# The last output tile of a spectral-mixing and MLP-mixer kernel: its products, sums, transposes and stores in another order and on three DMA queues

## The chip, the cores and the metric

The kernel runs on one core of a Trainium2 chip. The metric is device time in microseconds (us) for one execution; the number given for a kernel is the median of several unprofiled executions. A separate execution was profiled; its span runs from its first instruction to its last, and times inside it are counted from the span's start. Engines are named as the profile names them: PE is TensorE's matrix multiply and PEld its weight load, DVE is VectorE, ACT is ScalarE, POOL is GpSimd, SP is SyncE. A "q" after the name stands for the engine's sequencer: what it issues itself, such as DMAs and semaphore waits.

## The reference

```python
X = np.fft.rfft(x, axis=1)                      # x: 8 x 3008 x 256, fp32
y = np.fft.irfft(X * (filt_r + 1j * filt_i)[None], n=3008, axis=1)
h = np.maximum(y.transpose(0, 2, 1) @ w_tok1, 0.0) @ w_tok2     # token mixing
u = y + h.transpose(0, 2, 1)
out = u + np.maximum(u @ w_ch1, 0.0) @ w_ch2    # channel mixing, 256 -> 1536 -> 256
```

A filter in the frequency domain along the sequence is followed by an MLP over the 3008 tokens and an MLP over the 256 channels, each with a residual. All of it is fp32.

## The kernel before, in words

The Fourier transforms are products with small tables, done for groups of one or two batches (`GROUPS`). Their steps are a generator, `dft`, which the main loop advances at fixed places beside the mixer of an earlier batch, so that TensorE always has products to do. In the last batch there is no such work left.

The mixer (`mix`) goes over 8 batches, 6 tiles of tokens each (`MT`; the last tile of a batch has 448 tokens, the others 512) and 6 pairs of hidden channel blocks each (`JP`). One of these is an item `(b, m, jp)`. Products of 2 x 2 blocks are done with seven products in place of eight, so half-widths (256 or 224) and sums before and after appear everywhere. The loop is a software pipeline of depth two: in step `i` the first half of the channel MLP of item `i` (`up_first`, `up_middle`, `up_last`, the ReLU on ScalarE) stands between parts of the second half of item `i - 1` (`h_sums`, `down`). The instructions of each engine run in the order in which they are written, and waits on semaphores between engines come from the buffers that the instructions share.

`down` (L967 to L979) makes the seven products of an item in three parts, each of the form `po[i][:, j] += chan * mov`. Four PSUM banks `po[0]` to `po[3]`, each with two halves `j`, collect them over the six items of a tile. In the last item of a tile the order is (0,0), (0,1), (2,0), then (1,1), (3,0), then (2,1), (1,0). The operands are the ReLU's output `hh` and three kinds of sums of it, `t`, which VectorE makes in three operations (`h_sums`, through `v` at L922).

When a tile's last item is done, `finish` (L981 to L1029) adds the banks to the residual `u` (the tile `ut`, 2 x 448 or 2 x 512 per partition). It copies one half bank with ScalarE (L990) and makes eight additions on VectorE (`a`, `b_`, `c`, `d`). Two `transpose` instructions (L1010), one for each half of the channels (`dh`), turn 32 x 32 blocks into the tile `r`. The function `store` (L1012) then writes `r` with 16 DMAs (L1025): for `h` in 0, 1 (which of two token ranges), `e` in 0, 1 and `g` in 0 to 3 (blocks of 32 partitions). In every tile but the last of the last batch these are issued by GpSimd. In the last one SyncE and ScalarE issue eight each:

```python
last = b == B - 1 and m == MT - 1
q = (nc.sync, nc.scalar)[g % 2] if last else nc.gpsimd
```

For the very last tile there is no next item, so `down`, `finish` and `store` of it run with nothing beside them. After the program's last instruction come its end steps, which the profile puts at L1286, the line of the launch: SyncE waits for all DMAs and engines, each engine drains, GpSimd gathers the others in a barrier, semaphores are cleared, and a second barrier follows.

Of the kernel before, what the change touches and what calls it, by code (L numbers as in the profile page):

```python
# [10 lines left out]
FP32 = mybir.dt.float32  # L11
# [6 lines left out]
B = 8  # L18
N = 3008
N1 = 47  # L20
N2 = 64
NF = N // 2 + 1
D = 256
P = 128
K2 = 32
A = 24
KR = 4 * A
KH = KR // 2
HALF = 64
# [14 lines left out]
DH = D // P  # L44
CW = 32
CB = P // CW
MT = 6
# [80 lines left out]
def kernel(  # L128
# [11 lines left out]
    nc = tc.nc  # L140
# [19 lines left out]
    def pool(name, bufs, **kw):  # L160
        return ctx.enter_context(tc.tile_pool(name=name, bufs=bufs, **kw))
# [13 lines left out]
    tp = pool("tp", 2)  # L175
    vp = pool("vp", 2)
    sp = pool("sp", 1)
    rp = pool("rp", 1)
# [35 lines left out]
    chan = []  # L214
# [621 lines left out]
    def width(m):  # L836
        return 512 if m < MT - 1 else 448
# [83 lines left out]
    def v(out, in0, in1, op=ALU.add):  # L921
        nc.vector.tensor_tensor(out=out, in0=in0, in1=in1, op=op)  # L922

    def sums(t, b12_22, b11_12, b11, b21):

        return (lambda: v(t[:, 0:2], b12_22, b11_12, ALU.subtract),
                lambda: v(t[:, 2], t[:, 1], b11),
                lambda: v(t[:, 3], t[:, 2], b21, ALU.subtract))
# [6 lines left out]
    def h_sums(hh, t, w):  # L935

        h = hh[:, :, 0:w // 2]
        return sums(t[:, :, 0:w // 2], h[:, 1:3], h[:, 0:2], h[:, 0], h[:, 3])
# [28 lines left out]
    def down(m, jp, part, hh, t, po):  # L967
# [9 lines left out]
        for i, j, first, last, n, mov in todo[part]:  # L977
            nc.tensor.matmul(po[i][:, j, 0:hw], chan[1][:, jp, n, :], mov, start=(jp == 0 and first == 1),  # L978
                             stop=(jp == JP - 1 and last == 1))  # L979

    def finish(b, m, ut, po):  # L981

        w = width(m)
        hw = w // 2
        us = ut[:, :, 0:w].rearrange("p d (s n) -> p d s n", s=2)
        p23, p45, p16, p7 = (v_[:, :, 0:hw] for v_ in po)
        r = rp.tile([P, 512 // CW, DH, CW], FP32, tag="r", name="r")
        flat = r.rearrange("p k d i -> p (k d i)")
        p1, u2, u3 = (flat[:, ds(256 * i, hw)] for i in range(3))
        nc.scalar.copy(out=p1, in_=p16[:, 0])  # L990

        def a():
            v(us[:, 0], p23, us[:, 0])
            v(u2, p16[:, 1], p1)

        def b_():
            v(us[:, 1], p45, us[:, 1])
            v(us[:, 0, 1], p45[:, 1], us[:, 0, 1])
            v(u3, p7[:, 0], u2)

        def c():
            v(us[:, 0, 0], us[:, 0, 0], p1)
            v(us[:, 0, 1], us[:, 0, 1], u2)

        def d():
            v(us[:, 1], us[:, 1], u3.unsqueeze(1).to_broadcast([P, 2, hw]))

        def turn(dh):

            nc.vector.transpose(r[:, 0:w // CW, dh, :], ut[:, dh, 0:w].rearrange("p (k i) -> p k i", i=CW))  # L1010

        def store():  # L1012
            turn(1)
            ob = out[b]
            cw = DH * CW
            blocks = r.rearrange("p (q h e) d i -> p h e q (d i)", h=2, e=2)
            for h in range(2):
                n = min(4, (w - h * HALF + HALF) // P)
                for e in range(2):
                    for g in range(CB):  # L1020

                        last = b == B - 1 and m == MT - 1
                        q = (nc.sync, nc.scalar)[g % 2] if last else nc.gpsimd
                        row = e * 32 * N1 + (A + 4 * m if h else A - 1 - 4 * m)
                        q.dma_start(bass.AP(tensor=ob.tensor, offset=ob.offset + row * D + g * cw,  # L1025
                                            ap=[[N1 * D, 32], [D if h else -D, n], [1, cw]]),
                                    blocks[ts(g, CW), h, e, 0:n])

        return [a, b_, c, d, lambda: turn(0), store]  # L1029

    h1s, uts, vts = {}, {}, {}
# [22 lines left out]
    def mix(next_ready):  # L1054

        wait = []
        pos, hhs, tts = {}, {}, {}

        def loads(b):
            if b + 1 < B and next_ready(b):  # L1060
                for c in wait:
                    t4_load(b + 1, c)
                wait.clear()


        own = ({(4, 2): (0, 1)}, {(2, 2): (0,), (3, 0): (1,), (3, 2): (2, 3)})
        new = {(JP - 2, 0): (0, 1), (JP - 1, 0): (2, 3)}

        def u_parts(b, m, jp, place):
            parts = own[b > 0] if m + 1 < MT else new if b + 1 < B else {}  # L1070
            now = parts.get((jp, place), ())
            b, m = (b, m + 1) if m + 1 < MT else (b + 1, 0)
            for part in now:
                u_part(b, m, part)
            if now and now[-1] == max(p for ps in parts.values() for p in ps):
                if m:
                    wait.append(m)
                todo_v.extend(v_steps(b, m))
                if b and (b, m) < (B - 1, MT - 2):
                    w2m_load((m + 2) % MT)  # L1080

        to_dram = [f for m in range(MT) for f in w2_sums(m)]
        w1_todo, w1_out = w1_sums()
        items = [(b, m, jp) for b in range(B) for m in range(MT) for jp in range(JP)]
        n = MT * JP
        for i in range(len(items) + 1):
            now, old = i < len(items), i >= 1
            if JP - 2 <= i < JP + 2:
                for _ in range(6 if i > JP - 2 else 1):
                    if w1_todo:  # L1090
                        w1_todo.pop(0)()
            elif i >= 2 * JP and i % 2 and w1_out:
                w1_out.pop(0)()
            if i and ended[0] < len(tiles):
                convert_middle()
                convert_end(False)
                convert_middle()
            if now:
                b, m, jp = items[i]
                if i % n == 0:  # L1100
                    wait.append(0)
                w = width(m)
                hhs[i] = hp.tile([P, 4, 256], FP32, tag="hh", name="hh")
                g = [bank("pg").rearrange("p (s n) -> p s n", s=2) for _ in range(2)]
                s = up_first(jp, uts[b, m], vts[b, m], w, g)
                up_middle(hhs[i], w, g, s)
            while todo_h1:
                todo_h1.pop()()
            if i < n:
                one_step()  # L1110
            if old:
                bo, mo, jo = items[i - 1]
                tts[i - 1] = tp.tile([P, 4, 256], FP32, tag="t", name="t")
                for f in h_sums(hhs[i - 1], tts[i - 1], width(mo)):
                    f()
                down(mo, jo, 0, hhs[i - 1], tts[i - 1], pos.setdefault((bo, mo), []))
            if now:
                u_parts(b, m, jp, 0)
            copies()
            yield b, i % n, 0  # L1120
            if ended[0] < len(tiles):
                if i == 0:
                    convert_middle()
                convert_end(False)
            if now:
                up_last(jp, uts[b, m], vts[b, m], w, g, s, hhs[i])
                if b + 1 < B and i % n == n - 4:
                    t4_sums(b + 1, 0)
            one_step()
            if i >= n or i % n == n - 1:  # L1130
                one_step()
            if now and b + 1 < B:
                if n - 4 - W1S <= i % n < n - 4:
                    w1_load(i % n - (n - 4 - W1S))
                if i % n == n - 4:
                    t4_sums(b + 1, 1)
            copies()
            loads(b)
            yield b, i % n, 1
            if old:  # L1140
                down(mo, jo, 1, hhs[i - 1], tts[i - 1], pos[bo, mo])
            yield b, i % n, 1.5
            if old:
                down(mo, jo, 2, hhs.pop(i - 1), tts.pop(i - 1), pos[bo, mo])
                if jo == JP - 1:
                    todo_v.extend(finish(bo, mo, uts[bo, mo], pos[bo, mo]))
                    one_step()
                    one_step()
            if now:
                if b + 1 < B and i % n == n - 4:  # L1150
                    h1s[b + 1] = token_product(b + 1)
                u_parts(b, m, jp, 2)
                if jp == JP - 1:
                    while todo_v and m + 1 == MT:
                        one_step()
                if i >= 8 and to_dram:
                    to_dram.pop(0)()
                if i in (28, 29):
                    w2m_load(i - 28)
            loads(b)  # L1160
            yield b, i % n, 2
        while todo_v:
            one_step()

    with tc.manual_schedule():
# [69 lines left out]
        n = MT * JP  # L1235
        for b, i, place in mix(next_ready):
# [9 lines left out]
            jp = i % JP  # L1246
# [44 lines left out]
```

## Time and profile before

| what | value |
|---|---|
| median of 3 unprofiled executions | 2424.17 us (2424.15 to 2425.02) |
| the profiled execution's own time | 2425.85 us |
| its span, first to last instruction | 2424.1 us |
| mean granted TensorE clock | 0.995 |
| VectorE operations of 448 elements per partition (t, u, hh) | 0.61 to 0.63 us |
| VectorE operations of 224 elements per partition | 0.38 to 0.40 us |
| ScalarE copy of 224 elements (L990) | 0.35 us |
| DMAs of the last tile | 16, 32 KB or 24 KB each |

A row of the chain of work reads: start in us, duration in us, engine, tile and line, and how many instructions were merged. In the timeline a row is: start, duration, engine, line, operation, output and input tiles, count, and in brackets the idle time before it with what ended it. In a row of stretches the numbers after the length are, for each engine, the busy time and the count, then the granted clock, the mean busy share of the 16 DMA engines and the GB/s that they moved. In a row for one line and engine the durations are least, median and most in ns, followed by the first and last start in us.

### The profile page before, as it was taken

How to read it: one execution, taken by the hardware profiler on the slowest of the kernel's cores; microseconds unless marked ns; L12 is line 12 of the kernel's file. 1: busy time of each engine (PE TensorE's matmuls, PEld its weight loads, DVE VectorE, ACT ScalarE, POOL GpSimd, SP SyncE). 2: the span in 40 equal slices, each digit the busy share in tenths (PEclk: the TensorE clock that was granted, in tenths of full speed). 3: DMA queues.
4: the chain of work that ended last, by engine and by line, in shares of the span. 5: the costliest groups of instructions: out<-in, count | busy, mean ns of one | idle time of the engine just before them, and what ended most of it. 6: DMA issues, size and time to landing. Idle time of an engine off the chain costs nothing.

```text
span 2424.1 us, 35550 instructions
## 1 busy us (share of the span) xinstructions
PE 2382.0 (98%) x12340; PEld 1985.9 (82%) x12340; DVE 1942.6 (80%) x3684; ACT 686.5 (28%) x1355; POOL 619.6 (26%) x1115
## 2 busy tenths in 40 slices
PE   7999999999999999999999999999999999999998
PEld 4666676978888888987888888897889888898887
DVE  7798778787887888777888888877787788777776
ACT  5733322232222222123222222213221222222222
POOL 7476332113111211211121112112112112112121
PEclk8999999999999999999999999999999999999999
DMA  9975545544343322444344222434324221411100
GB/s 217 248 231 166 155 144 177 161 155 138 108 133 98 86 79 78 160 134 146 103 132 125 76 81 82 145 101 133 90 75 151 63 60 46 152 63 31 39 15 20
DMA packets 187420, 278.66 MB, mean 115 GB/s; under 512 B 35485, under 2 KB 125291, under 8 KB 187240
## 3 DMA queue, kind: packets, MB, share of 16 engines
q1 hardware_dynamic: 140952, 212.56, 29.1%
q0 software_dynamic: 34688, 53.83, 8.2%
q10 hardware_dynamic: 11600, 10.00, 1.3%
q8 instruction: 98, 1.61, 0.3%
q14 instruction: 82, 0.67, 0.1%
HBM read 193.52 MB, written 82.72 MB: 114 GB/s over the span
## 4 chain that ended last, share of the span: by engine, by line
PE 90%; DVE 4%; DMA 2%; ACT 1%; issue 1%; POOL 1%; SPq 0%; ACTq 0%; DVEq 0%; POOLq 0%
PE ps_po L978 33%; PE ps_pg L944 18%; PE ps_pg L960 14%; PE ps_b L523 4%; PE ps_b L810 3%; PE ps_acc L865 3%; PE ps_acc L810 2%; PE ps_b L865 2%; PE ps_b L843 2%; PE ps_acc L843 2%; PE ps_pg L523 1%; PE ps_b L759 1%; DVE t L922 1%; DVE hh L922 1%; DMA filt<-in_x_dram 1%
## 5 line engine op out<-in xcount | busy, mean ns | idle before, releaser
L1025 POOL DMA_DIRECT2D out_dram<-r x752 | 407.9, 550 | 1542.3 <-issue 1082.2
L922 DVE TENSOR_TENSOR hh<-ps_pg,s 128x512 f32<-128x512 f32 (+3 forms) x864 | 482.0, 585 | 184.3 <-ACT s L947 181.4
L965 ACT ACTIVATE hh<-hh 128x512 f32<-128x512 f32 (+1 forms) x576 | 347.7, 621 | 993.4 <-DVE hh L922 989.5
L978 PE MATMUL ps_po<-t,wc 128*128 128x256 f32 (+1 forms) x2304 | 553.5, 379 | 1.8 <-DVE t L922 1.8
L978 PEld LDWEIGHTS ps_po<-t,wc 128*128 128x128 f32 x2304 | 427.8, 190 | 122.6 <-issue 40.8
L978 PE MATMUL ps_po<-hh,wc 128*128 128x256 f32 (+1 forms) x1728 | 413.2, 375 | 1.0 <-POOL wc L382 0.8
L944 PE MATMUL ps_pg<-v,wc 128*128 128x256 f32 (+1 forms) x1728 | 413.3, 375 | 0.7 <-POOL wc L381 0.7
L944 PEld LDWEIGHTS ps_pg<-v,wc 128*128 128x128 f32 x1728 | 327.3, 190 | 41.3 <-DVE v L922 3.1
L978 PEld LDWEIGHTS ps_po<-hh,wc 128*128 128x128 f32 x1728 | 327.7, 190 | 39.6 <-POOL wc L382 2.0
L960 PE MATMUL ps_pg<-u,wc 128*128 128x256 f32 (+1 forms) x1152 | 292.9, 377 | 1.2 <-DVE hh L922 1.2
L922 DVE TENSOR_TENSOR t<-t,hh 128x256 f32<-128x256 f32 (+1 forms) x576 | 245.0, 425 | 19.8
L960 PEld LDWEIGHTS ps_pg<-u,wc 128*128 128x128 f32 x1152 | 216.7, 190 | 44.2 <-DVE hh L922 13.9
L922 DVE TENSOR_TENSOR s<-ps_pg,hh 128x512 f32<-128x512 f32 (+1 forms) x288 | 196.1, 681 | 30.0
L947 ACT COPY s<-ps_pg 128x256 f32<-128x256 f32 (+1 forms) x288 | 105.9, 368 | 362.7 <-PE ps_pg L944 360.5
L922 DVE TENSOR_TENSOR t<-hh 128x512 f32<-128x512 f32 (+1 forms) x288 | 195.0, 677 | 0.6 <-ACT hh L965 0.6
L944 PE MATMUL ps_pg<-u,wc 128*128 128x256 f32 (+1 forms) x576 | 169.3, 375 | 2.9 <-DVE hh L922 2.8
L960 PE MATMUL ps_pg<-v,wc 128*128 128x256 f32 (+1 forms) x576 | 168.8, 375 | 0.0
L944 PEld LDWEIGHTS ps_pg<-u,wc 128*128 128x128 f32 x576 | 108.1, 190 | 19.3 <-DVE hh L922 6.2
L922 DVE TENSOR_TENSOR u<-ps_acc,u 128x256 f32<-128x256 f32 (+1 forms) x84 | 46.2, 550 | 97.0 <-PE ps_acc L865 66.1
L960 PEld LDWEIGHTS ps_pg<-v,wc 128*128 128x128 f32 x576 | 109.1, 190 | 12.7
L922 DVE TENSOR_TENSOR u<-ps_b,u 128x512 f32<-128x512 f32 (+2 forms) x126 | 74.4, 591 | 28.9 <-PE ps_b L865 26.7
L865 PE MATMUL ps_acc<-w 128*128 128x256 f32 (+1 forms) x336 | 85.5, 377 | 1.0 <-ACT t L539 1.0
(152 smaller groups left out, 2661.9 us busy)
## 6 DMA issues: line engine op xcount, KB each, us to landing
w<-w_tmp SPq DMA_DIRECT2D x84, 448.0 KB
w<-w_tmp SPq DMA_DIRECT2D x35, 896.0 KB
out_dram<-r POOLq DMA_DIRECT2D x696, 32.0 KB, 2.5
t<-g_tmp SPq DMA_DIRECT2D x42, 512.0 KB
g_tmp<-t SPq DMA_DIRECT2D x96, 192.0 KB
t<-z_tmp SPq DMA_DIRECT2D x180, 96.0 KB
z_tmp<-t SPq DMA_DIRECT2D x60, 256.0 KB
filt<-in_x_dram SPq DMA_DIRECT2D x90, 128.0 KB
```

What stands on the lines that cost most here:

```text
L523: nc.tensor.matmul(outs(i, j), stat(i, j), mov(i, j), start=True, stop=True)
L759: nc.tensor.matmul(acc[:, t, :], w1[:, a, ts(t, P)], t4[b, a // TC4][:, a % TC4, :], start=(a == 0 and t == 0), stop=(a == A - 1 and t == ...
L810: nc.tensor.matmul(ps[:, at], w[:, n], mov, start=(j == 0 and i in (0, 2)), stop=(j == AP - 1 and i >= 5))
L843: nc.tensor.matmul(ps[:, ds(q * P, n)], t4[b, c][:, r, ts(dh, P)], wai[:, 0:n], start=(first and q == 0), stop=(not first and q == 3))
L865: nc.tensor.matmul(ps[:, ds(j * hw, hw)], h1[:, n, :], w2m[m % 2][:, at, 0:hw], start=(i < 2 and j == 0), stop=(j == len(todo) - 1))
L922: nc.vector.tensor_tensor(out=out, in0=in0, in1=in1, op=op)
L944: nc.tensor.matmul(ps[:, 0:hw], chan[0][:, jp, n, :], mov, start=True, stop=True)
L947: nc.scalar.copy(out=s[:, 0], in_=g[0][:, 0, 0:hw])
L960: nc.tensor.matmul(ps[:, 0:hw], chan[0][:, jp, n, :], mov, start=True, stop=True)
L965: nc.scalar.activation(out=hs, in_=hs, func=AF.Relu)
L978: nc.tensor.matmul(po[i][:, j, 0:hw], chan[1][:, jp, n, :], mov, start=(jp == 0 and first == 1), stop=(jp == JP - 1 and last == 1))
L1025: q.dma_start(bass.AP(tensor=ob.tensor, offset=ob.offset + row * D + g * cw, ap=[[N1 * D, 32], [D if h else -D, n], [1, cw]]), blocks[ts(g ...
```

## The change

In the step after the last item, the loop calls a new function, `last_item`, and ends. The items before it, and `finish` for the other 47 tiles, are as they were; `store` only moves its DMAs into a helper, `store_piece`, with GpSimd as the queue for all of them.

`last_item` does for the very last item what `h_sums`, `down` and `finish` did, in this order. The seven products are (0,0), (0,1), (2,0), (1,1), (2,1), (3,0), (1,0). The partial sums lie in a tile `s` of the pool `sp` in place of the space of `r`. The sums on VectorE are seven operations, the first as before. The transposes are cut into eight: for each `h` and `e`, one for each `dh`, of 128 elements for `h` = 0 and 96 for `h` = 1. The four stores of a group `(h, e)` follow its two transposes. Of these, two go to one hardware queue, one to the other and one to GpSimd; in sum ScalarE and SyncE issue six each and GpSimd four.

```diff
+    def store_piece(b, m, blocks, h, e, n, queues):
+        ob = out[b]
+        cw = DH * CW
+        row = e * 32 * N1 + (A + 4 * m if h else A - 1 - 4 * m)
+        for g, q in enumerate(queues):
+            q.dma_start(bass.AP(tensor=ob.tensor, offset=ob.offset + row * D + g * cw,
+                                ap=[[N1 * D, 32], [D if h else -D, n], [1, cw]]),
+                        blocks[ts(g, CW), h, e, 0:n])
+
+    def last_item(b, m, jp, hh, t, ut, po):
+        w = width(m)
+        hw = w // 2
+        b11, b21, b22 = (hh[:, i, 0:hw] for i in (0, 3, 2))
+        t1, t3, t2, t4_ = (t[:, i, 0:hw] for i in range(4))
+
+        def times(i, j, last, n, mov):
+            nc.tensor.matmul(po[i][:, j, 0:hw], chan[1][:, jp, n, :], mov, start=False, stop=last)
+
+        for f in h_sums(hh, t, w):
+            f()
+        times(0, 0, False, 1, b21)
+        times(0, 1, True, 2, b22)
+        times(2, 0, False, 0, b11)
+        times(1, 1, False, 6, t1)
+        times(2, 1, True, 5, t2)
+        times(3, 0, True, 4, t3)
+        times(1, 0, True, 3, t4_)
+        us = ut[:, :, 0:w].rearrange("p d (s n) -> p d s n", s=2)
+        p23, p45, p16, p7 = (v_[:, :, 0:hw] for v_ in po)
+        u = sp.tile([P, 3, 256], FP32, tag="s", name="s")[:, :, 0:hw]
+        nc.scalar.copy(out=u[:, 0], in_=p16[:, 0])
+        v(us[:, 0], p23, us[:, 0])
+        v(u[:, 1], p16[:, 1], u[:, 0])
+        v(us[:, 0], us[:, 0], u[:, 0:2])
+        v(u[:, 2], p7[:, 0], u[:, 1])
+        v(us[:, 1], us[:, 1], u[:, 2].unsqueeze(1).to_broadcast([P, 2, hw]))
+        v(us[:, :, 1], us[:, :, 1], p45[:, 1].unsqueeze(1).to_broadcast([P, 2, hw]))
+        v(us[:, 1, 0], us[:, 1, 0], p45[:, 0])
+        r = rp.tile([P, 512 // CW, DH, CW], FP32, tag="r", name="r")
+        blocks = r.rearrange("p (q h e) d i -> p h e q (d i)", h=2, e=2)
+        for h in range(2):
+            n = min(4, (w - h * HALF + HALF) // P)
+            for e in range(2):
+                for dh in range(DH):
+                    rows = ut[:, dh].rearrange("p (q h e i) -> p h e q i", h=2, e=2, i=CW)
+                    nc.vector.transpose(blocks[:, h, e, 0:n, ts(dh, CW)], rows[:, h, e, 0:n])
+                hw_queues = (nc.sync, nc.scalar) if e else (nc.scalar, nc.sync)
+                store_piece(b, m, blocks, h, e, n, [hw_queues[0], hw_queues[1], nc.gpsimd, hw_queues[0]])
...
                 for e in range(2):
-                    for g in range(CB):
-
-                        last = b == B - 1 and m == MT - 1
-                        q = (nc.sync, nc.scalar)[g % 2] if last else nc.gpsimd
-                        row = e * 32 * N1 + (A + 4 * m if h else A - 1 - 4 * m)
-                        q.dma_start(bass.AP(tensor=ob.tensor, offset=ob.offset + row * D + g * cw,
-                                            ap=[[N1 * D, 32], [D if h else -D, n], [1, cw]]),
-                                    blocks[ts(g, CW), h, e, 0:n])
+                    store_piece(b, m, blocks, h, e, n, [nc.gpsimd] * CB)
...
             now, old = i < len(items), i >= 1
+            if not now:
+                bo, mo, jo = items[i - 1]
+                t = tp.tile([P, 4, 256], FP32, tag="t", name="t")
+                last_item(bo, mo, jo, hhs.pop(i - 1), t, uts[bo, mo], pos[bo, mo])
+                break
```

More of the change, by code (lines that the diff above doesn't have):

```diff
@@ L1013, in store @@
             turn(1)
-            ob = out[b]
-            cw = DH * CW
             blocks = r.rearrange("p (q h e) d i -> p h e q (d i)", h=2, e=2)
```

## The prediction

> **What bounds the kernel now.** First the page's busy times. TensorE is busy 98% of the span, so over the whole run nothing but its work counts; the change leaves all but the last seven products alone.
>
> ```profile
> PE 2382.0 (98%) x12340; PEld 1985.9 (82%) x12340; DVE 1942.6 (80%) x3684; ACT 686.5 (28%) x1355; POOL 619.6 (26%) x1115
> ```
>
> Second, the chain of work that ended last, cut to the end of the span (start us, us, what). After the last products nothing is left for TensorE, and every step is in the open.
>
> ```profile
> 2410.84 2.55 PE ps_po L978 x12
> 2413.39 0.02 issue
> 2413.41 0.35 ACT r L990
> 2413.77 0.02 issue
> 2413.79 0.39 DVE r L922
> 2414.18 0.83 DVE u L922 x2
> 2415.01 0.30 DVE r L922
> 2415.30 1.15 DVE u L922 x3
> 2416.45 0.02 issue
> 2416.47 0.65 DVE r L1010
> 2417.12 0.53 DVEq L1286
> ```
>
> Each product is two instructions here, 0.19 us apart. ScalarE's copy at 2413.41 reads only what the third product wrote, yet it waits for twelve instructions, six products: the sixth is the last into the same bank (po2), so the wait goes by bank. Then VectorE works alone until 2417.65 (2.68 us of sums, 1.17 of two transposes).
>
> Third, the timeline after that, and the busy times by stretches (the last three numbers: TensorE clock, DMA share, GB/s).
>
> ```profile
> 2417.72 3.81 ACTq L1025 DMA_DIRECT2D out_dram<-r  x8
> 2417.74 3.69 SPq L1025 DMA_DIRECT2D out_dram<-r  x8
> ```
> ```profile
> 2418.50:2420.50 2.00, 0.00 (x0) 0.00 (x0) 0.00 (x0) 0.00 (x0) 0.00 (x0) 0.56 0.63 131
> 2420.50:2422.40 1.90, 0.00 (x0) 0.00 (x0) 0.00 (x0) 0.00 (x0) 0.00 (x0) 0.50 0.51 104
> 2422.40:2424.10 1.70, 0.00 (x0) 0.00 (x0) 0.00 (x0) 0.00 (x0) 0.00 (x0) 0.50 0.00 0
> ```
>
> The stores are bound by their issue: 0.48 us each on ScalarE's queue, 0.46 on SyncE's, while the DMA engines are 63% and then 51% busy. The last issue starts at 2421.1; SyncE, done issuing at 2421.4, then waits 1.2 for a transfer, so the last lands near 2422.7, 1.65 after its issue began. 1.4 us of end-of-program steps follow (L1286, the launch line) to 2424.1.
>
> Fourth, GpSimd, which ends its own part early now. Its timeline, its end-of-program drain (ns, start us) and, for comparison, VectorE's:
>
> ```profile
> 2396.06 8.66 POOL L1025 DMA_DIRECT2D out_dram<-r  x16 [30.42 <-ACT s L947]
> ```
> ```profile
> L1286 POOLq DRAIN  x1: 9032/9032/9032, 2402.9 to 2402.9; - x1
> ```
> ```profile
> L1286 DVEq DRAIN  x1: 1207/1207/1207, 2416.5 to 2416.5; - x1
> ```
>
> The sixteen stores of the tile before are all issued by 2396.06 + 8.66 = 2404.72, the last landing 2.6 after its start at 2404.16, at 2406.7. But the drain that follows in GpSimd's order ends only at 2402.95 + 9.03 = 2411.98: 7.27 us after the last issue, 5.3 after the last landing. VectorE's drain ends 0.05 after its last transpose. Today this costs nothing, because 2411.98 lies 11 us ahead of the final barrier, in which GpSimd gathers the others (its first semaphore there: 2423.3, then 0.77 to the end).
>
> [...]
>
> **The change, part by part.** All times are in the profiled run, span 2424.1 inside 2425.85 us; the unprofiled median is 2424.17. I work with differences and add them to the median.
>
> *Order of products.* (2,1), the last into po2, moves from sixth to fifth. Its operand t2 is ready at 2411.88 (the t rows: 2411.48 and 2 x 0.41), ahead of its slot at 2410.84 + 8 x 0.19 = 2412.4, so no stall. Copy at 2413.41 - 0.38 = 2413.03, done 2413.38: **-0.38**. The bounds are 0 and -0.38.
>
> *Sums.* From the rows, an operation starts 0.53 (448 elements) or 0.30 (224) after an independent one, but 0.65 or 0.42 after one it depends on. Before, after the first sum: seven operations, 2413.79 to 2416.47, 2.68. After, six: u1 2413.41; us0 + u 2413.83 (dependent); u2 2414.36; us1 + u2 2414.78 (dependent); the strided sum with p45 2415.43 (dependent); the last 224 2415.96; first transpose 2416.26. That is 2.85: one operation fewer, but more of them dependent, **+0.17**. The swapped operand order and the strided output I cost at nothing, since rows of 448 take 614 to 616 ns whether their operands lie in PSUM or in SBUF; at worst 0.1.
>
> *Transposes.* Two of 448 become four of 128 and four of 96 elements. The trace has none so small; [...] The nearest row, a 128x128 tensor_tensor at 292 ns, agrees. Bounds: 0.15 and 0.35 apart. Groups are ready at 2416.76, 2417.17, 2417.52, 2417.86: the whole is 0.22 later than now (2417.65), the first group 0.89 **earlier**.
>
> *Hardware queues.* Six issues each instead of eight, the first at 2416.84 (0.08 after the transpose, as now). ScalarE's sixth starts at 2416.84 + 5 x 0.48 = 2419.24, SyncE's at 2419.2; no group is late for them. Eight completion semaphores take turns, so the fifth on a queue waits for the landing of the first: 2416.84 + 1.65 = 2418.49 against 2418.76, as now with nothing to spare beyond 0.3; bounds 0 and +0.5. Last landing 2419.24 + 1.65 = 2420.89: **-1.85** against 2422.74.
>
> *GpSimd's four.* Each waits for its group on VectorE, with nothing behind it but the drain. The earlier tile's sixteen stand ahead of it and have landed. GpSimd starts late: the earlier tile's transposes end at 2395.49 and its first store starts at 2396.06, 0.57 after. So 2416.76 + 0.57, then 0.54 apart (8.66/16): 2417.33, 2417.86, 2418.40, 2418.94, ending 2419.49. Landing 1.8 after (quiet median) or up to 3.3: 2420.7 to 2422.2. As transfers these four are level with the hardware queues. DMA load: 16 engines spent 0.63 x 2.0 + 0.51 x 1.9 = 2.2 us on all stores; squeezed into 3.4 us that fits.
>
> *GpSimd's drain, now last.* The four issues put the drain behind 2419.49. If its delay is fixed from the last issue, it ends at 2419.49 + 7.27 = 2426.76; if from the last landing, at 2420.7 + 5.3 = 2426.0. With 0.77 of barrier: 2427.5 or 2426.8. Below: if it is proportional to the stores queued (7.27 for sixteen), four cost 1.8, ending 2421.3, under cover of the landings. I take the fixed delay, because GpSimd's ordinary operations start right behind such a train of stores elsewhere in this trace (one at 292.42 as sixteen stores end at 292.41), so no backlog of unfinished stores stands behind it.
>
> **Sum:** without the drain, -1.85 and some 0.1 for contention; with it, 2427.5 - 2424.1 = **+3.4**. Forecast 2424.17 + 3.4 = 2427.6, its own range 2426.4 to 2428.4.
>
> **Rivals.** *A, the drain stays hidden* (proportional to queued stores, or a one-time cost that only began with sixteen of them). Then the last landing ends the kernel: 2420.9 to 2421.3, plus 1.2, 2422.3; -1.8 gives **2422.4**. For it: one drain alone is in the trace. Against it: a drain free of backlog should have ended as VectorE's did. It decides as soon as the delay after the last issue is under 2421.4 - 2419.5 = 1.9 us. *B, no change:* the drain hidden, and small transposes at 0.35 apart (ready 1.2 later at the end) and semaphore turns (+0.5) eat the gain: **2424.0**. Against it: the 292 ns row. *C, drain fixed and the landings slow too* (the last three stores of the tile before took up to 3.3, beside an instruction fetch): 2422.2 + 5.3 + 0.77 = 2428.3, median **2428.7** or more.
>
> **Numbers.** Forecast 0.62, A 0.27, B 0.05, C 0.06. The forecast alone holds too little, so the range reaches to A: 2422.2 to 2428.4, leaving out C and the edges. All cases lie within 0.2% (4.85 us: 2419.3 to 2429.0), about what a measurement of this kernel can tell from no change, so "same" takes 0.93, slower 0.05 (C's upper part), faster 0.02.
>
> **What would show it.** GpSimd's drain at the launch line ending some 7 us after its last store, and nothing else in the last 4 us: right. SyncE's last wait on a transfer ending past GpSimd's drain: A. Each step: copy at 2413.0, first transpose at 2416.3, first issues at 2416.8, last hardware issue at 2419.2[...]. A drain delay that scales with four stores in sixteen would make the forecast wrong in sign.

## The result, and the profile after

The changed kernel takes 2429.35 us (median of 20 runs, 2427.01 to 2432.39) against 2424.89 for the kernel before, run beside it (20 runs, 2422.69 to 2427.19): ratio 1.0017, 95% interval 1.0011 to 1.0023, that is 4.1 us slower (2.7 to 5.6). The forecast was 2427.6 and its range ended at 2428.4. The profiled execution has a span of 2427.4 us, the span worked out was 2427.5; so close an agreement is in part luck, since the last seven products started 0.36 earlier than in the profile before.

Both programs are the same until the last seven products, and these start at different times in different executions of one program (between 2408.0 and 2414.5 us in the twelve profiles of this study). So the profiles are compared by their *tail*: from the start of the first of the seven products to the end of the span. Before it is 2424.07 - 2410.84 = 13.23 us, after 2427.415 - 2410.478 = **16.94**: +3.70. "At tail 6.37" below means 6.37 us after that start.

The busy times are those of before; nothing of the change shows in them.

```profile
PE 2380.4 (98%) x12340; PEld 1984.6 (82%) x12340; DVE 1944.7 (80%) x3689; ACT 686.6 (28%) x1355; POOL 624.1 (26%) x1119
```

The timeline from the seven products on:

```profile
2410.48 1.40 PE L997 MATMUL ps_po<-hh,wc 128*128 128x224 f32 x6 [0.16 <-ACT hh L965]
...
2412.73 0.35 ACT L1011 COPY s<-ps_po 128x224 f32<-128x224 f32 x1 [2.30 <-PE ps_po L997]
2413.11 0.39 DVE L922 TENSOR_TENSOR s<-ps_po,s 128x224 f32<-128x224 f32 x1 [0.64 <-ACT s L1011]
2413.53 0.62 DVE L922 TENSOR_TENSOR u<-u,s 128x448 f32<-128x448 f32 x1
2414.07 0.38 DVE L922 TENSOR_TENSOR s<-ps_po,s 128x224 f32<-128x224 f32 x1
2414.49 0.62 DVE L922 TENSOR_TENSOR u<-u,s 128x448 f32<-128x448 f32 x1
2415.22 0.92 DVE L922 TENSOR_TENSOR u<-u,ps_po 128x448 f32<-128x448 f32 x2
2416.06 1.52 DVE L1026 STREAM_TRANSPOSE r<-u 128x128 f32<-128x128 f32 x8
2416.58 2.89 SPq L986 DMA_DIRECT2D out_dram<-r  x6
2416.59 3.15 ACTq L986 DMA_DIRECT2D out_dram<-r  x6
2416.85 2.18 POOL L986 DMA_DIRECT2D out_dram<-r  x4 [12.46 <-DVE r L1026]
```

All that was meant to move has moved: the first store is issued at tail 6.10 (before: 6.88, its 2417.72), the last issue on a hardware queue ends at tail 9.26 (2416.59 + 3.15; before 10.69), and the queues carry six, six and four.

Then comes GpSimd's drain, its row at the line of the launch (ns, start us), and the busy times by stretches (the last three numbers are clock, DMA share, GB/s):

```profile
L1330 POOLq DRAIN  x1: 8218/8218/8218, 2418.4 to 2418.4; - x1
```
```profile
2417.40:2420.50 3.10, 0.00 (x0) 0.00 (x0) 0.18 (x2) 0.00 (x0) 1.63 (x4) 0.71 0.75 148
2420.50:2421.30 0.80, 0.00 (x0) 0.00 (x0) 0.00 (x0) 0.00 (x0) 0.00 (x0) 0.50 0.00 0
2421.30:2427.40 6.10, 0.00 (x0) 0.00 (x0) 0.00 (x0) 0.00 (x0) 0.00 (x0) 0.50 0.00 0
```

In the first stretch the DMA engines are busier than before (75% against the 63% of the stretch shown ahead), and they move the last byte by 2420.5. From there no engine computes and no transfer runs for 6.9 us, where the kernel before had 1.7. The drain ends at 2418.405 + 8.218 = 2426.62: 7.59 after GpSimd's last issue (2416.85 + 2.18 = 2419.03), and 5.41 after the landing of its last store. The chain of waits and SyncE's waits (us in total, times, longest) read:

```profile
2417.93 0.56 POOL out_dram L986
2418.49 0.54 POOLq L1330
```
```profile
SPq L1330 <- PEq L1330: 5.4, 2, 4.9
SPq L1330 <- DMA out_dram<-r: 1.8, 3, 0.8
SPq L986 <- DMA out_dram<-r: 0.3, 1, 0.3
```

The chain ends on GpSimd's issues, so its sequencer closes the program. The waits need care: 5.4 us are put down to TensorE's sequencer, yet TensorE's last product ends at 2413.4. Before, the same line had 0.7 us. The only thing that lasts through those 4.9 us is GpSimd's drain. The third line is a stall of SyncE's sixth store, which the prediction had costed at nothing.

A GpSimd row ends well before its data has landed: rows of 0.55 us, landings 2.0 to 2.7 us after their start.

### The profile page after: what moved, and what is told of

It is laid out like the page before. It is cut to its first block, busy times and chain, and to the rows that moved or that the text cites. A ratio compares the mean times of both kernels' runs of the same rounds, so it can differ in the third digit from the quotient of the medians.

```text
span 2427.4 us, 35563 instructions
## 1 busy us (share of the span) xinstructions
PE 2380.4 (98%) x12340; PEld 1984.6 (82%) x12340; DVE 1944.7 (80%) x3689; ACT 686.6 (28%) x1355; POOL 624.1 (26%) x1119
## 4 chain that ended last, share of the span: by engine, by line
PE 87%; DVE 5%; DMA 3%; issue 2%; POOL 1%; ACT 1%; SPq 0%; ACTq 0%; DVEq 0%; POOLq 0%
PE ps_po L978 33%; PE ps_pg L944 18%; PE ps_pg L960 14%; PE ps_b L523 4%; PE ps_b L810 3%; PE ps_acc L865 3%; PE ps_acc L810 2%; PE ps_b L865 2%; PE ps_b L843 2%; PE ps_acc L843 2%; PE ps_pg L523 1%; DVE t L922 1%; DVE hh L922 1%; DMA st<-in_moe_w_tok_dram 1%; DMA x<-in_x_dram 1%
```

## The experiments

The theory is that of the forecast: GpSimd's drain stands behind its new stores and costs about 7.3 us from the last of them. The rivals: the order of products, the cut sums and transposes or the three queues cost the time themselves; the drain is bound by landings; or its length comes from something else than "a store in front of it". The kernel before ran beside them at 2425.97 us (46 runs, first four kernels), 2426.04 (17 runs, next three) and 2426.02 (25 runs, last three). Every kernel here computes the whole reference.

**1. The change without GpSimd.** In the changed kernel:

```diff
-store_piece(b, m, blocks, h, e, n, [hw_queues[0], hw_queues[1], nc.gpsimd, hw_queues[0]])
+store_piece(b, m, blocks, h, e, n, [hw_queues[0], hw_queues[1], hw_queues[0], hw_queues[1]])
```

> The changed kernel, but GpSimd's four stores of the last tile go to SyncE and ScalarE, eight each. Measure: the tail, from the start of the first of the last seven products to the end of the span; it is 13.2 us before and 16.9 us after the change. Theory D (GpSimd's drain, some 7.4 us behind its last issue, sets the end): the drain is early again; first issue at 6.1, eighth at 6.1 + 7 x 0.48 = 9.5, landing 1.65 later, 1.35 of end steps: tail 12.5, about 4.4 less than after, 0.7 less than before. Theory Q (the new order of sums, small transposes or semaphore turns lose the time): tail stays at 16 or more.

Measured: 2425.25 us, ratio 0.9994 (0.9986 to 1.0003), tail 12.45. Timeline and drain:

```profile
2416.88 3.71 SPq L986 DMA_DIRECT2D out_dram<-r  x8
2416.88 3.79 ACTq L986 DMA_DIRECT2D out_dram<-r  x8
```
```profile
L1330 POOLq DRAIN  x1: 9035/9035/9035, 2402.9 to 2402.9; - x1
```

With the drain back at 2402.9, ending at 2411.9 under the last products, the tail is 0.78 *shorter* than before. So new order, sums, transposes and finer groups are a small gain, and the four GpSimd stores cost 16.94 - 12.45 = 4.5 us.

**2. One store on GpSimd in the kernel before.** Nothing else of the change:

```diff
-q = (nc.sync, nc.scalar)[g % 2] if last else nc.gpsimd
+q = (nc.sync, nc.scalar)[g % 2] if last and (h, e, g) != (0, 0, 2) else nc.gpsimd
```

> The kernel before, with one of the last tile's sixteen stores (h 0, e 0, g 2) on GpSimd. Theory D with a fixed delay: the one issue ends at about 7.9 us of the tail, the drain 7.4 later, 0.75 of barrier: tail 16.1, 2.9 more than before. Theory P (the drain's time is proportional to the stores it follows, 7.3 us for sixteen): 0.5 us, hidden: tail 13.2 or a little less.

Measured: 2429.64 us, ratio 1.0012 (1.0004 to 1.002), tail 16.06. The timeline's GpSimd row and the drain:

```profile
2419.05 0.55 POOL L1025 DMA_DIRECT2D out_dram<-r  x1 [13.49 <-issue]
```
```profile
L1286 POOLq DRAIN  x1: 7919/7919/7919, 2419.0 to 2419.0; - x1
```

One store of 32 KB is enough: +2.83 of tail. The drain ends 7.35 us after this one issue. A length proportional to the stores of the last tile is out.

**3. Four stores on GpSimd in the kernel before.**

```diff
+q = (nc.sync, nc.scalar, nc.gpsimd, nc.scalar if e else nc.sync)[g] if last else nc.gpsimd
```

> The kernel before, with four of the last tile's sixteen stores (g 2 of each group) on GpSimd and six each on the other queues; sums and transposes as before. Theory D fixed: last GpSimd issue ends at 7.4 + 4 x 0.54 = 9.5, drain to 16.9, tail 17.7, 4.5 more than before. Theory P: drain 1.8 us, hidden; two issues fewer on each hardware queue: tail 12.3.

Measured: 2430.22 us, ratio 1.0017 (1.001 to 1.0024), tail 17.93; the drain is 8400 ns long and ends 7.59 after the last issue, 5.98 after the last landing. In the changed kernel these are 7.59 and 5.41. Counted from the last *issue* the delay is the same, from the landing it is not: here landings don't set it. The queues without the finer groups lose 4.7 us; the finer groups, first ready at tail 6.1 in place of 6.9, give 1.0 of that back.

**4. A drain ahead of the last item.** One line at the start of `last_item` in the changed kernel, so that GpSimd drains once while TensorE and VectorE still work:

```diff
+        nc.gpsimd.drain()
```

> The changed kernel with one more GpSimd drain, put between the sixteen stores of the tile before and the four of the last tile; it runs beside the last products and should end before the first transpose does. Theory D with a delay for every drain that follows stores: both drains take their 7 us, tail 16.9 as after. Theory W (a one-time cost, of the first drain in a long while or of all the stores issued since): the last drain is short (under 2 us), the last landing ends the kernel, tail 12.0.

Measured: 2425.27 us, ratio 0.9998 (0.9989 to 1.0006), tail 12.18. The two drains, the added one first:

```profile
L999 POOLq DRAIN  x1: 9027/9027/9027, 2404.6 to 2404.6; - x1
```
```profile
L1331 POOLq DRAIN  x1: 2947/2947/2947, 2420.4 to 2420.4; - x1
```

The added drain takes the long delay (7.26 after the last issue before it). The one at the end, behind the same four stores, ends 2.34 after the last issue and 0.22 after the last landing. So the forecast's *fixed* delay of each drain behind a store is wrong: something accumulates during the program, and the first drain pays for it. The kernel that remains is the changed one with its penalty hidden: its tail is 1.05 under that of before.

**5. The same with two stores on GpSimd** (kernel 4, and in the groups of `h` = 0 alone a store on GpSimd):

```diff
+[hw_queues[0], hw_queues[1], hw_queues[0] if h else nc.gpsimd, hw_queues[h]]
```

> A version meant to beat both: the drain ahead of the last tile's stores as in the run with the drain first, and GpSimd issues only one store in each of the first two groups; SyncE and ScalarE issue seven each. Last hardware issue at 6.1 + 6 x 0.47 = 8.9 of the tail, landing near 10.7, GpSimd's landing before it: tail 12.0, against 13.2 before, 12.2 with four stores. If semaphore turns cost 0.3 to 0.4 on these queues too: 12.4.

Measured: 2425.15 us, ratio 0.9994 (0.9986 to 1.0002), tail 12.16, last drain 2516 ns, ending 0.13 after the last landing. There is nothing to choose between two stores and four once the penalty is hidden.

**6. What accumulates? A drain one tile earlier,** in `store` of the last tile but one, ahead of its stores:

```diff
+            if (b, m) == (B - 1, MT - 2):
+                nc.gpsimd.drain()
```

> The changed kernel with one more GpSimd drain ahead of the sixteen stores of the tile before the last, so that 20 stores stand between it and the last drain, some 45 us apart. Tail measured as before: 16.9 us in the changed kernel, 12.2 with the drain right ahead of the last four stores. Theory B (the drain works off all stores issued since the last drain, 947 in the changed kernel's case, some 7.3 us for them): 20 stores cost 0.15 us, last drain ends with the last landing, tail 12.2. Theory O (a drain's first use in a long while costs 7 us, and a use some us ago makes the next one cheap): 12.2 too if 45 us are short, 16.9 if they are long.

Measured (one execution): tail 12.35. The added drain and the last:

```profile
L1063 POOLq DRAIN  x1: 7757/7757/7757, 2363.2 to 2363.2; - x1
```
```profile
L1332 POOLq DRAIN  x1: 3638/3638/3638, 2418.1 to 2418.1; - x1
```

The added one, behind 935 of GpSimd's DMAs instead of 951, ends 5.96 after the last issue; the last, with 20 DMAs since, 0.87 after the last landing.

**7. A drain after 583 DMAs** (the condition above with `(4, 0)`):

> The changed kernel with one more GpSimd drain in the first tile of batch 4, with 388 stores and some other transfers of GpSimd between it and the last one, over 1100 us apart. Theory B, proportional: 7.3 x 390 / 950 = 3.0 us behind the last issue, only just past the last landing: tail 12.2 to 12.8, and the early drain some 4 us. Theory B with a bound [...]: the full 7.4 us, tail 16.9. Theory O, one time only in the program: tail 12.2. Theory O with a use that is forgotten: tail 16.9.

Measured (one execution): tail 13.49. The drain in the middle and the one at the end:

```profile
L1063 POOLq DRAIN  x1: 5547/5547/5547, 1370.3 to 1370.3; - x1
```
```profile
L1332 POOLq DRAIN  x1: 4780/4780/4780, 2420.3 to 2420.3; - x1
```

The first ends 3.84 after the last issue, the second 4.16 after it, with 372 DMAs since, all of them stores (the expectation's 388 is too many). Only the early drain of "some 4 us" came as expected; no version gives the tail. A one-time cost is out, since both drains are long. So is proportion to all DMAs: 583 cost 3.84, and 372 cost more. What fits is that only some of the DMAs count (the next expectations call those that don't *retired*, a word for the fit; which ones count is taken up behind the next two kernels). Between 935 and 955 DMAs the drain grows by (7.59 - 5.96)/20 = 0.082 us for each. At that price 7.59 us is some 92 of 955 DMAs, and 5.96 some 72 of 935: by this estimate the first 863 cost nothing.

**8 and 9. A test of that count.** Some tiles of the last batch store by SyncE, so that GpSimd issues fewer DMAs before the last four, 875 and 923 in all (the expectations call all of them stores; 199 are other loads and copies):

```diff
-store_piece(b, m, blocks, h, e, n, [nc.gpsimd] * CB)
+store_piece(b, m, blocks, h, e, n, [nc.sync if b == B - 1 else nc.gpsimd] * CB)        # 8
+store_piece(b, m, blocks, h, e, n, [nc.sync if (b, m) >= (B - 1, 3) else nc.gpsimd] * CB)   # 9
```

> The changed kernel, but five of the six tiles of the last batch ahead of the last one (80 stores) go out on SyncE's queue. GpSimd then issues 875 stores in all instead of 955, the last four of them still at the end. Theory N (the drain costs 0.082 us for each GpSimd store that is not yet retired, and the first 863 or so retire on their own): some 12 are left, the drain would take 1.0 us after the last issue and so is bound by the last landing instead, ending 0.2 to 0.9 us after it; tail from the start of the last seven products 12.0 to 12.7 us. Theory F (a fixed delay of 7.3 to 7.6 us behind the last issue whenever GpSimd stores come last): tail 16.9 us, span as in the changed kernel. Theory P (proportional to all stores issued, 875/955): drain 6.95 us after the last issue, tail 16.3.

> As the run before it in this list, but only the two tiles of the last batch ahead of the last one (32 stores) go out on SyncE's queue; GpSimd issues 923 stores in all. Theory N: some 60 are left at the end, 60 x 0.082 = 4.9 us after the last issue, tail 8.55 + 4.9 + 0.8 = 14.3 us. Theory F: 16.9 us. Theory P: 923/955 of 7.59, 7.3 us after the last issue, tail 16.7.

Measured (one execution each): tails 11.88 and 14.32. The timeline's row and the drain, kernel 8:

```profile
2419.10 2.19 POOL L986 DMA_DIRECT2D out_dram<-r  x4 [214.25 <-DVE r L1026]
```
```profile
L1330 POOLq DRAIN  x1: 2992/2992/2992, 2420.7 to 2420.7; - x1
```

and kernel 9:

```profile
2417.41 2.18 POOL L986 DMA_DIRECT2D out_dram<-r  x4 [92.63 <-DVE r L1026]
```
```profile
L1330 POOLq DRAIN  x1: 5599/5599/5599, 2419.0 to 2419.0; - x1
```

With 60 counted, 4.9 us was expected after the last issue and 4.98 is measured; with 12 counted, a drain bound by the landing, and it ends 0.54 after GpSimd's last. A fixed delay (tail 16.9) and proportion to all (16.3 and 16.7) are both out. The idle time in brackets says one thing more: in kernel 9 GpSimd issued nothing for 92 us, and the 56 older DMAs in the count (60 less the new four) still cost their full price. Time alone doesn't take them out of the count. Kernel 8's tail is a little under its expectation (12.0): its last stores are stalled less (ScalarE's sixth starts at tail 8.56, not 8.94) and land earlier (at 10.79, not 11.15).

| drain | DMAs | counted (less 863) | ends after last issue, us | 0.082 x counted |
|---|---|---|---|---|
| 6, added | 935 | 72 | 5.96 | 5.90 |
| kernel before; 4, added | 951 | 88 | 7.27; 7.26 | 7.22 |
| 2 | 952 | 89 | 7.35 | 7.30 |
| changed; 3; 10 | 955 | 92 | 7.59; 7.59; 7.59 | 7.54 |
| 9 | 923 | 60 | 4.98 | 4.92 |

The first and fourth rows gave the price and the 863; the ninth kernel is the test. The delay repeats to 0.01 us wherever the count is the same, so one execution shows it. It goes by DMAs and not by bytes: two of the changed kernel's four stores are of 24 KB, and the four add 7.59 - 7.27 = 0.32, 4 x 0.082, where by bytes it would be 3.5 x 0.082 = 0.29.

Few counted DMAs don't hide behind the landing altogether: the drain ends 0.13, 0.22, 0.54 and 0.87 us after GpSimd's last landing for 2, 4, 12 and 20 (kernels 5, 4, 8, 6), which is 0.05 + 0.041 for each, half the price. So one sum, fitted to these runs, gives the ends of all sixteen drains that stand behind GpSimd's DMAs, to 0.02 us: take the later of the last landing and 0.041 n after the last issue, n being the count, and add 0.041 n + 0.05. For 92 that is 7.59 after the last issue, for 20 (landing 2.14 after it) 3.01, both as measured. In kernels 4, 5 and 6 a drain stands shortly ahead and n is known without the 863.

The traces also show where the count starts. In all twelve profiles GpSimd pauses for 1.4 to 3.0 us, between two stores of one tile, ahead of its DMAs number 225, 329, 437 and 545, and in all but kernel 7 ahead of 653, 761 and 871. In kernel 7 the drain behind number 583 moved the later pauses to 699, 807 and 915. The brackets show two of them, the pause ahead of 871 in kernel 8 and the one ahead of 699 in kernel 7:

```profile
2204.30 0.55 POOL L986 DMA_DIRECT2D out_dram<-r  x1 [1.65 <-issue]
```
```profile
1738.07 7.03 POOL L986 DMA_DIRECT2D out_dram<-r  x13 [2.38 <-issue]
```

The count starts eight ahead of the last pause: 871 - 8 = 863, the number found above without the pauses. In kernel 7, 545 - 8 = 537 leaves 46 of 583, and 915 - 8 = 907 leaves 48 of 955; the sum gives 3.82 and 4.16 for them, where 3.84 and 4.16 were measured. So the old DMAs go out of the count at these pauses, as far as the agreement of these three counts shows it. What GpSimd does in a pause, and why pauses lie some 108 stores apart, no trace shows. Kernel 8 pays so little because its last four stores come just behind one.

**10. The changed kernel again,** unedited, because the medians in the first comparison differ by 2429.35 - 2424.89 = 4.46 and the tails by 3.70.

> The changed kernel again, unedited, beside the kernel before on one chip. If the change costs only what its tail shows (16.94 against 13.23 us from the start of the last seven products), the ratio is 1.0015 (+3.7 us). If something ahead of the tail is slower too, the ratio is again 1.0018 or more (+4.4 us and over) with the lower end of the interval above 1.0015.

Measured: 2429.2 us (21 runs), ratio 1.0014 (1.0008 to 1.0021), +3.4 us; tail 16.93. The tail repeats to 0.01 us, and 3.7 lies in both intervals. The surplus of 0.8 in the first comparison is scatter; nothing speaks for a loss ahead of the tail.

## Why the prediction was wrong on the time, and right on the place

The path of the forecast is what happens: GpSimd's drain, moved behind its new stores, ends the program. The working of the tail came within 0.25 us. The reason that it gave for the drain's length was wrong, and that the length came out close is luck: four more DMAs hardly change a count of 88. In tail times (the forecast's less 2410.84):

| step | forecast | measured |
|---|---|---|
| copy starts | 2.19 | 2.25 |
| first sum starts | 2.57 | 2.63 |
| first transpose starts | 5.42 | 5.58 |
| first hardware issue | 6.00 | 6.10 |
| last hardware issue | 8.40 | 8.94 |
| GpSimd's first issue | 6.49 | 6.37 |
| GpSimd's last issue ended | 8.65 | 8.55 |
| drain ends | 15.92 | 16.14 |
| span ends | 16.69 | 16.94 |

*Order of products.* Right: the copy waits for the fifth product. It gained 0.32, not 0.38.

*Sums.* 2.95 from first sum to first transpose, not 2.85. The strided sum was costed at nothing; it starts 0.73 after the sum it depends on (2415.22 - 2414.49), where 0.65 was the distance before. The first transpose is late by 0.16, which passes on to GpSimd's first store. That store starts 0.29 after the transposes that it waits for, where 0.57 was taken; the two errors nearly cancel (6.37 against 6.49), which is luck.

*Transposes.* From the first start to the last end they take 1.52 us, where the forecast had 1.60 (2416.26 to 2417.86). That was the author's estimate, with a tensor_tensor of 128x128 at 292 ns as its nearest row; the transposes of 128 elements average 277 ns and those of 96 take 234. They start 0.16 to 0.23 apart, so rival B's 0.35 is out.

*Hardware queues.* Here the step was wrong that put the semaphore turns at nothing and every landing at 1.65. ScalarE's sixth store is stalled by 0.42 us and SyncE's by 0.30, inside the bounds of 0 to 0.5 that the text kept. Each waits for the landing of the second store on its queue: ScalarE's second lands at 2419.34, 2.3 us after its start, and its sixth starts at 2419.42; SyncE's second lands at 2419.14 and its sixth starts at 2419.16. That is invisible in the changed kernel, but it is why kernel 4 gains 1.05 and not rival A's 1.8: there ScalarE's sixth store starts at tail 8.91 and lands 2.18 later, at 11.09, where rival A had at most 10.46. GpSimd's last landing, at 10.67, is earlier. In kernel 1, with eight stores on each hardware queue and none on GpSimd, the last one lands at 11.11. So the third queue by itself brought the landings forward by 0.02 us. What kernel 4 has over kernel 1 lies behind the last landing: SyncE has three waits left there and seven in kernel 1, 0.06 us each.

*GpSimd's four.* Start and spacing right within 0.12, the start by the luck just told.

*The drain.* Place and sign right, the term mis-sized by 0.32: the 7.27 us from the last issue became 7.59, because four more DMAs cost 4 x 0.082 = 0.33. The reason given for it, a fixed delay with no backlog behind it, fell: behind fewer counted DMAs the drain after the same four stores ended 4.98 (kernel 9) and 2.36 us (kernel 8) after the last issue. That GpSimd's ordinary operations start right behind a train of stores shows that the issues are over, not how long a drain behind them takes. Rival A's reason, proportion, was nearer to the truth, yet its number wasn't, since what counts is not the four stores of one tile but, by the fit, 92 DMAs: all since eight ahead of the last pause. A one-time cost the 7.27 is not either, since the length goes by the count of DMAs (7.59 for 92, 4.98 for 60).

*The base and the range.* This is the step that failed. The error is 2429.35 - 2427.6 = 1.75 us. The drain and the smaller terms of the tail give 3.70 - 3.43 = 0.27. "I work with differences and add them to the median" gives 0.72: that median, 2424.17, came from three runs, and twenty give 2424.89; with the other chips, 2425.97 to 2426.04. The last 0.76 is the scatter of this comparison (kernel 10). The three runs lay within 0.9 us and twenty spread over 4.5. The sign was on the page: the profiled execution, of the same program, took 2425.85, outside the three. A term for the base of about 1 us either way belonged in the range, whose top stood only 0.8 above the forecast. A slip stands beside it: rival C's 2428.3 is a time in the span of 2424.1, so its median is 2424.17 + 4.2 = 2428.4 and not 2428.7; the range left out a case that lay at its top. That all cases lie "within 0.2%" of the kernel before holds: 0.17%.

## What to carry to other kernels

Before giving an idle engine a share of the last work, look at what that engine does *after* its last work: its end-of-program steps move with it, as GpSimd's drain did here from 2402.9 to 2418.4. A queue that is done early may hide a long drain, and here a single 32 KB store uncovered 2.8 us; where a drain shows such a cost, keep GpSimd's DMAs out of the last few microseconds, or let it drain once while others work (tail 12.18 in kernel 4, 16.94 without). And take the base of a forecast from its scatter, the profiled execution's own time included, when the effect is as small as the scatter.

## What the runs showed of the hardware

GpSimd's drain is not constant. With nothing to wait for, drains took 7 ns on SyncE and 19 on VectorE in the last barrier. The drain behind GpSimd's DMAs took 2.5 to 9.0 us (kernels 5 and 1), and in the fit to these runs its end goes by a count of them: 0.082 us for each from the last issue, or, where the landing comes later, 0.041 us for each from there, with 0.05 more. Up to 92 counted.

A drain in the course of the program clears the count: behind one, the same four stores had a drain that ended 2.34 us after the last issue, not 7.59. So, as far as twelve traces show, does a pause of GpSimd's own of 1.4 to 3.0 us, for all but the eight DMAs ahead of it; behind DMA 329 it came every 108 of them, once after 110. Time alone doesn't: 56 DMAs were still counted after 92 us without any.

No version beats the kernel before by what can be measured: the tails of kernels 1, 4 and 5 (12.16 to 12.45) are 0.8 to 1.1 us under it, 0.03 to 0.04%, and the intervals of their ratios hold 1. Kernel 8's tail of 11.88 comes from one execution.
